# Regrouping the KV matmuls of a linear-attention kernel by array shape, and one identity made earlier

## The chip, the cores and the metric

The kernel runs on one core of one Trainium2 chip. The metric is the device time of one execution in microseconds (us), the median of several runs. Within a core five engines run side by side, each through its own instructions in order: TensorE (PE in the profile, its weight loads PEld), VectorE (DVE), ScalarE (ACT), GpSimd (POOL) and SyncE (SP). They wait for each other through semaphores.

## The reference, cut to what matters

Shapes: batch 8, heads 8, sequence 576, head dimension 64, features 128 (with both signs 256).

```python
def phi(x):
    proj = np.einsum('bhsd,df->bhsf', x, w_phi)
    proj = proj - np.max(np.abs(proj), axis=-1, keepdims=True)
    return np.concatenate([np.exp(proj), np.exp(-proj)], axis=-1)
q_p, k_p = (phi(q), phi(k))
kv = np.einsum('bhsf,bhsd->bhfd', k_p, v)
z = np.sum(k_p, axis=2)
num = np.einsum('bhsf,bhfd->bhsd', q_p, kv)
den = np.einsum('bhsf,bhf->bhs', q_p, z)[..., None] + 1e-06
x = num / den            # heads side by side: (8, 576, 512)
gate = 1 / (1 + exp(-causal_conv5(x, conv_w)))
out = (gate * (x @ w_val)) @ w_out
```

The KV sums are `kv` and `z`: for each batch, head and sign a product of 128 features by 65 columns (64 of v and a column that gives z), summed over 576 tokens.

## The kernel before, in words

A unit is two batches (b = 0, 1) and two heads (h = 0, 1); there are 16 units, four for each of the four pairs of batches. A unit's tokens lie in nine blocks of 128 partitions per head. The two batches have 576 tokens each, four blocks and a half, so blocks 0 to 3 belong to batch 0, blocks 5 to 8 to batch 1, and block 4 is shared: batch 0 in partitions 0 to 63, batch 1 in partitions 64 to 127.

The work is staged by hand. A step handles one of three groups (g = 0, 1, 2) of three blocks of a unit; each step issues its parts in the order `"KkTtNVxQLnaCvXqdc"`, in which capital letters stand for TensorE work and the others mostly for the engine that reads the result. In one step, for different units:

- K, k, x: `pe_K` (L260) projects keys into the PSUM tile PK; `max_K` (L268, VectorE) takes the row maxima MK; `exp_K` (L273, ScalarE) writes the key features KTIL with two exp activations, one for each sign.
- T, t: `pe_T` (L241, and L244 for the query maxima MQb) transposes the next group's KN and QN with the bf16 identity `ident_bf`; `copy_T` (L254, VectorE) copies to QKT.
- N, n: `pe_N` (L353) makes numerator and denominator NUM, `norm` (L361, L364, VectorE) divides, giving XN, seven steps behind K.
- V, v: `pe_KV` (L332, L335), once per unit, at the third group of the unit four steps back, makes the KV sums; `copy_KV` (L343, VectorE) copies them to KVSB in bf16.
- Q, q: `pe_Q` (L260, tile PA) and `max_Q` (L283, VectorE) make the query maxima MQb.
- L, a, d: the gated unit's work of a finished pair as a budget allows: GATE (L419), VAL (L440) and OP (L448) on TensorE, the tanh GS (L425) and the copy OS (L453) on ScalarE, the product GV (L429) on VectorE.
- C, c: `pe_C` (L306, L311, tile PQ) and `exp_C` (L318, ScalarE) make the query features QTIL, three steps behind K.
- X: once per pair, the transposes XP (L383) and their copies XT (L393, VectorE).

After the third group of a unit `emit_VT` lets GpSimd scale v by the keys' maxima: VT0 for the first sign, VT1 for the second (L294, L296).

PSUM is shared out in two pools: `ps2` has three buffers of two banks, which PK, PA, PQ, KV and GATE take in the order in which they are requested, and `ps1` two buffers of one bank, for T, NUM, XP, VAL and OP. A buffer can be written again once its last reader is done.

In `pe_KV` a two-bank tile holds batch 0 in one bank and batch 1 in the other, and in each bank four accumulators of 65 columns, n = 2h + sign. For each n the old order does four whole-array matmuls (128 partitions) for batch 0, four for batch 1, and then block 4: two matmuls on 64 partitions each, one for each batch, which take the upper and the lower half of the array. `start` clears the bank's flags, so that the first write to an accumulator overwrites.

At the start GpSimd issues the loads of unit 0 (`load_two(0)`, L123 and L129: four DMAs of KN, two of QN, four of VN), then makes the two identities `ident_bf` and `ident_f` (a memset and a select each, inside the helper masks.py), then issues unit 1's loads. VectorE makes EB (L166), ident_2 (L189) and DIAG (L195) from `ident_f`; TensorE transposes the convolution's weights with it (cwps, L192). This part stands ahead of the manual schedule, and the framework orders it by readiness.

Of the kernel before, what the change touches and what calls it, by code (L numbers as in the profile page):

```python
# [23 lines left out]
NC = NG * GC  # L24
# [32 lines left out]
def kernel(  # L57
# [24 lines left out]
    nc = tc.nc  # L82
# [14 lines left out]
    def half(h):  # L97
        return slice(h * D, h * D + D)

    def two_banks(name):  # L100
        return ps2.tile([P, 2, 512], FP32, name=name, tag="b2")
# [6 lines left out]
    for j, pr in enumerate(pairs):  # L108
        pr.j = j
        for hp in range(NHP):  # L110
            u = _Unit()
# [3 lines left out]
    def load_hps(j, tiles, hp0, nhp, dst0):  # L115
        QN, KN, VN = tiles
        h0, nh = 2 * hp0, 2 * nhp
        hs, ds = slice(h0, h0 + nh), slice(dst0, dst0 + nh)
        b0, b1 = 2 * j, 2 * j + 1
        lo, hi = slice(0, D), slice(D, P)  # L120
        def qload():
            for bb, ps in ((b0, lo), (b1, hi)):
                nc.gpsimd.dma_start(QN[ps, ds, :, :],  # L123
                                    q[bb, hs].rearrange("h (p c) d -> p h c d", c=NC))
        def kvload(T, x):
            for bb, ps, t0, nt, c0 in ((b0, lo, 0, 320, 0), (b0, hi, 320, 256, 0),
                                       (b1, lo, 0, 256, 5), (b1, hi, 256, 320, 4)):
                n = nt // D
                nc.gpsimd.dma_start(T[ps, ds, c0:c0 + n, :],  # L129
                                    x[bb, hs, t0:t0 + nt].rearrange("h (p c) d -> p h c d", c=n))  # L130
        kvload(KN, k)
        qload()
        kvload(VN, v)

    def load_two(i):

        u0, u1 = units[2 * i], units[2 * i + 1]
        tiles = [ldp.tile([P, 4, NC, D], BF16, name=n) for n in ("QN", "KN", "VN")]
        for w, u in enumerate((u0, u1)):
            u.QN, u.KN, u.VN = (t[:, 2 * w:2 * w + 2] for t in tiles)  # L140
        if i == 0:
            load_hps(u0.j, tiles, u0.hp, 1, 0)
            u1.load = lambda: load_hps(u1.j, tiles, u1.hp, 1, 2)
        else:
            load_hps(u0.j, tiles, u0.hp, 2, 0)


    load_two(0)
    ident_bf = const.tile([P, P], BF16, name="ident_bf")
    make_identity(nc, ident_bf[:])  # L150
    ident_f = const.tile([P, P], FP32, name="ident_f")
    make_identity(nc, ident_f[:])

# [169 lines left out]
    def pe_KV(u):  # L323
        KV = two_banks("KV")
        kvv = KV[:, :, 0:4 * (D + 1)].rearrange("p b (n e) -> p b n e", e=D + 1)
        for h in range(2):
            for sg in range(2):
                n = 2 * h + sg
                for b in range(2):
                    for c in range(4):  # L330
                        cc = c + 5 * b
                        nc.tensor.matmul(kvv[:, b, n, :], u.KTIL[:, sg, h * NC + cc, :], u.VT[sg][:, h * NC + cc, :],  # L332
                                         start=(c == 0), stop=False)
                for b in range(2):
                    nc.tensor.matmul(kvv[:, b, n, :], u.KTIL[half(b), sg, h * NC + 4, :],  # L335
                                     u.VT[sg][half(b), h * NC + 4, :],
                                     start=False, stop=True)
        u.KVps = kvv

    def copy_KV(u):  # L340
# [151 lines left out]
    def step(t):  # L492
# [18 lines left out]
        for o in ORDER:  # L511
            if o == "K" and u: pe_K(u, g)
            elif o == "k" and u: max_K(u, g)
            elif o == "x" and u: exp_K(u, g)
            elif o == "T" and (un or um): tt = pe_T(un, gn, um)
            elif o == "t" and (un or um): copy_T(un, um, *tt)
            elif o == "Q" and u: pe_Q(u, g)
            elif o == "q" and u: max_Q(u, g)
            elif o == "C" and uc: pe_C(uc, gc)
            elif o == "c" and uc: exp_C(uc, gc)  # L520
            elif o == "V" and uv and gv == 2: pe_KV(uv)
            elif o == "v" and uv and gv == 2: copy_KV(uv)
            elif o == "N" and ux: pe_N(ux, gx)
            elif o == "n" and ux:
                norm(ux, gx)
            elif o == "X" and uy and uy.hp == NHP - 1:
                for n in range(gy * GC, gy * GC + GC):
                    copy_X(uy.pair, n, pe_X(uy.pair, n))
                if gy == 1:
                    emit_virt(uy.pair, 0)  # L530
                if gy == 2:
                    emit_virt(uy.pair, 1)
                    ready[t + LAGM] = uy.pair
            elif o == "L":
                budget = min(budget + BUDGET[g], 45)
                while mlp and budget > 0:
                    cost, f = mlp.pop(0)
                    later.extend(f())
                    budget -= cost
            elif o == "a": run_later(ACT_)  # L540
            elif o == "d": run_later(DVE_)
# [46 lines left out]
```

## Time and profile before

| what | value |
|---|---|
| time, median of 3 runs | 280.35 us (279.16 to 280.41) |
| profiled execution | 279.15 us, of which 277.4 us are the span of the program's instructions |
| busy share of the span | TensorE 83%, VectorE 71%, ScalarE 66%, GpSimd 51% |
| TensorE instructions in all | 3488 matmuls, 3508 weight loads recorded |
| `pe_KV`, whole-array matmuls (L332) | 512, mean 198 ns each as drawn |
| `pe_KV`, half-row matmuls (L335) | 128, mean 203 ns each as drawn |
| VectorE's wait for the KV sums (L343) | 11.4 us in 16 waits |

The profile is that of one execution. A line of a timeline gives the start from the beginning of the span, the duration, the engine, the line of the kernel, the operation, the tile written and those read, the shape, and the number of instructions merged into it; a bracket at its end gives the idle time of the engine before it and what ended it. Matmuls are pipelined: each is drawn longer than the step from one start to the next, so TensorE's pace is read from starts. The chain of waits is followed back from the last instruction, at each step to what released it.

### The profile page before, as it was taken

To read this page: it belongs to the slowest core of one execution; us is meant where nothing else is said; L and a number is where in the kernel's file an instruction comes from. 1 tells how busy PE (TensorE), PEld (TensorE's weight loads), DVE (VectorE), ACT (ScalarE), POOL (GpSimd) and SP (SyncE) were. 2 spreads that over 40 slices of the span, in tenths; PEclk is the share of its full clock that TensorE was granted. 3 is DMA by queue.
4 is the path that set the end of the run, shared out by engine and by line. 5 is a ranking of instruction groups with operands and counts; after the bars stand their busy time and mean duration, and the time that the engine had idled before them with its cause. 6 is when DMAs were issued, how large, how long until landed. Compare 5 with 4: busy or idle time off the path is not lost.

```text
span 277.4 us, 8159 instructions
## 1 busy us (share of the span) xinstructions
PE 230.2 (83%) x3488; PEld 147.2 (53%) x3508; DVE 195.8 (71%) x346; ACT 182.7 (66%) x281; POOL 142.4 (51%) x195
## 2 busy tenths in 40 slices
PE   0478977777889989897899989998799989869992
PEld 0345755665655556575656464766546455533441
DVE  0798699999897667878897488778977554453211
ACT  1079798898666875979566786978648758202451
POOL 8999969969920946087714934143506051030000
PEclk9999999999999999999999999999999999988998
DMA  6999995934930497339900894411001503310445
GB/s 86 135 143 187 188 158 79 175 48 58 154 50 0 83 210 118 78 79 147 150 2 1 138 216 61 113 40 40 2 2 35 120 2 91 73 32 0 99 106 138
DMA packets 28990, 25.24 MB, mean 91 GB/s; under 512 B 2709, under 2 KB 24341, under 8 KB 28954
## 3 DMA queue, kind: packets, MB, share of 16 engines
q0 software_dynamic: 23024, 15.21, 39.9%
q1 hardware_dynamic: 5930, 9.52, 14.2%
q8 instruction: 27, 0.44, 0.7%
q14 instruction: 9, 0.07, 0.1%
HBM read 30.48 MB, written 9.44 MB: 144 GB/s over the span
## 4 chain that ended last, share of the span: by engine, by line
PE 55%; DVE 25%; ACT 12%; POOL 3%; issue 3%; POOLq 0%; ACTq 0%; DVEq 0%
PE OP L448 12%; PE GATE L419 8%; PE VAL L440 8%; PE KV L332 8%; DVE MK L268 8%; ACT KTIL L273 5%; DVE MQb L283 5%; PE NUM L353 4%; ACT QTIL L318 4%; DVE QKT L254 3%; PE KV L335 3%; PE XP L383 2%; PE PK L260 2%; PE T L241 2%; DVE GV L429 2%
## 5 line engine op out<-in xcount | busy, mean ns | idle before, releaser
L294 POOL TENSOR_TENSOR VT<-VN,E 128x1152 bf16<-128x1152 bf16 x32 | 68.7, 2149 | 78.5 <-issue 67.8
L273 ACT ACTIVATE KTIL<-PK 128x768 bf16<-128x768 f32 x96 | 73.1, 822 | 27.6 <-DVE MK L268 27.5
L318 ACT ACTIVATE QTIL<-PQ 128x768 bf16<-128x768 f32 x96 | 73.2, 826 | 18.9 <-PE PQ L311 18.9
L268 DVE TENSOR_REDUCE MK<-PK 128x6 f32<-128x768 f32 x48 | 45.9, 956 | 9.0 <-PE PK L260 8.9
L429 DVE SCALAR_TENSOR_TENSOR GV<-GS,VAL 128x512 bf16<-128x512 bf16 (+1 forms) x40 | 24.8, 633 | 37.8 <-ACT GS L425 32.8
L283 DVE TENSOR_REDUCE MQb<-PA 128x6 bf16<-128x768 f32 x48 | 45.6, 951 | 0.0
L448 PE MATMUL OP<-WOUT,GV 128*128 128x512 bf16 x124 | 33.9, 380 | 4.8 <-DVE QKT L254 3.3
L425 ACT ACTIVATE GS<-GATE 128x1024 bf16<-128x1024 f32 (+1 forms) x20 | 18.8, 939 | 26.0 <-PE GATE L419 25.6
L440 PE MATMUL VAL<-XT,WVAL 128*128 128x512 bf16 (+1 forms) x192 | 35.0, 329 | 0.0
L453 ACT ACTIVATE OS<-OP 128x512 f32<-128x512 f32 x36 | 21.8, 607 | 17.4 <-PE OP L448 13.3
L260 PEld LDWEIGHTS <-QKT 64*128 64x128 bf16 x576 | 20.1, 98 | 23.3 <-issue 13.5
L260 PE MATMUL PK<-W,QKT 64*128 64x128 bf16 x288 | 17.4, 229 | 16.5 <-ACT KTIL L273 10.3
L353 PE MATMUL NUM<-KVSB,QTIL 128*128 128x65 bf16 (+1 forms) x640 | 29.9, 196 | 0.5 <-DVE XT L393 0.3
L332 PE MATMUL KV<-VT,KTIL 128*128 128x65 bf16 x512 | 28.0, 198 | 0.0
L364 DVE TENSOR_TENSOR XN<-NUM,RCP 128x384 bf16<-128x384 f32 x48 | 26.8, 558 | 1.7
L254 DVE COPY QKT<-T 128x768 bf16<-128x768 bf16 (+2 forms) x49 | 27.5, 562 | 0.3 <-PE T L244 0.3
L353 PEld LDWEIGHTS <-QTIL 128*128 128x128 bf16 (+1 forms) x640 | 24.6, 100 | 3.2 <-issue 0.7
L419 PE MATMUL GATE<-XT,DIAG 64*64 64x512 bf16 (+1 forms) x480 | 24.6, 337 | 1.2 <-POOL XT L400 1.2
L440 PEld LDWEIGHTS <-WVAL 128*128 128x128 bf16 x192 | 14.9, 98 | 19.0 <-issue 7.5
L241 PE MATMUL T<-ident_bf,KN 128*128 128x128 bf16 x144 | 23.9, 236 | 0.0
L241 PE MATMUL T<-ident_bf,QN 128*128 128x128 bf16 x144 | 23.6, 235 | 0.0
L129 POOL DMA_DIRECT2D KN<-in_k_dram x36 | 22.7, 667 | 0.8 <-POOLq L572 0.8
(45 smaller groups left out, 298.2 us busy)
## 6 DMA issues: line engine op xcount, KB each, us to landing
out_dram<-OS SPq DMA_DIRECT2D x72, 128.0 KB, 2.4
QN<-in_q_dram POOLq DMA_DIRECT2D x14, 288.0 KB, 7.2
KN<-in_k_dram POOLq DMA_DIRECT2D x14, 160.0 KB, 4.5
VN<-in_v_dram POOLq DMA_DIRECT2D x14, 160.0 KB, 8.6
KN<-in_k_dram POOLq DMA_DIRECT2D x14, 128.0 KB, 4.4
VN<-in_v_dram POOLq DMA_DIRECT2D x14, 128.0 KB, 8.5
QN<-in_q_dram POOLq DMA_DIRECT2D x4, 144.0 KB, 3.7
WNAT<-in_moe_w_val_dram POOLq DMA_DIRECT2D x1, 512.0 KB, 6.2
```

The costliest lines, as they stand in the source:

```text
L241: nc.tensor.transpose(T[:, s * GC + i, :], src.rearrange("p h c d -> p (h c d)")[:, m * P:(m + 1) * P], ident_bf[:, :])
L260: nc.tensor.matmul(PA[:, r, i * P:(i + 1) * P], u.T[g][half(r), s, i, :], W2[half(r), :], start=True, stop=True)
L268: nc.vector.tensor_reduce(u.MK[:, :].rearrange("p (m r) -> p r m", r=2)[:, :, blocks(g)], u.PK, AX.X, ALU.max, apply_absolute_value=True)
L273: nc.scalar.activation(u.KTIL[:, sg].rearrange("p (m r) f -> p r m f", r=2)[:, :, blocks(g), :], u.PK, AF.Exp, scale=1.0 - 2.0 * sg)
L283: nc.vector.tensor_reduce(mq, u.PA, AX.X, ALU.max, apply_absolute_value=True, negate=True)
L294: nc.gpsimd.tensor_tensor(VT[:, :, 0:D], u.VN.rearrange("p h c d -> p (h c) d"), eb.to_broadcast([P, 2 * NC, D]), ALU.mult)
L318: nc.scalar.activation(u.QTIL[:, sg, :, :, g * GC * D:(g + 1) * GC * D], PQ[:, :, 0:GT].rearrange("p r (b x) -> p r b x", b=2), AF.Exp, sc ...
L332: nc.tensor.matmul(kvv[:, b, n, :], u.KTIL[:, sg, h * NC + cc, :], u.VT[sg][:, h * NC + cc, :], start=(c == 0), stop=False)
L353: nc.tensor.matmul(NUM[ps, i, h, :], u.QTIL[:, sg, r, b, m * D:m * D + ps.stop - ps.start], u.KVSB[:, b, 2 * h + sg, :], start=(sg == 0), ...
L419: nc.tensor.matmul(GATE[half(c), r, z * n:(z + 1) * n], DIAG[half(r), jt, tap, :], cols(jt, 4 - tap, half(r)), start=(tap == 0), stop=(tap ...
L440: nc.tensor.matmul(VL[:, z, :], WVAL[:, dt, v * P:(v + 1) * P], cols(dt, 0), start=(dt == 0), stop=(dt == 3))
L448: nc.tensor.matmul(OP[:, :], pr.GV[g][:, jt // 2, jt % 2, i * P:(i + 1) * P], WOUT[:, jt, :], start=(jt == 0), stop=(jt == 3))
```

## The change

In `pe_KV` all 32 whole-array matmuls of a unit come first, block by block (c), within a block over the four accumulators n, within these over the two batches b, so that successive matmuls write to alternating banks. The eight half-row matmuls come after them. `start` is set only for the first matmul into each bank. The numbers of matmuls and of weight loads are unchanged. Apart from this, `ident_bf` is made before `load_two(0)` in place of after it.

```diff
-    load_two(0)
     ident_bf = const.tile([P, P], BF16, name="ident_bf")
     make_identity(nc, ident_bf[:])
+    load_two(0)
     ident_f = const.tile([P, P], FP32, name="ident_f")
     make_identity(nc, ident_f[:])
...
     def pe_KV(u):
         KV = two_banks("KV")
         kvv = KV[:, :, 0:4 * (D + 1)].rearrange("p b (n e) -> p b n e", e=D + 1)
-        for h in range(2):
-            for sg in range(2):
-                n = 2 * h + sg
+
+        for c in range(4):
+            for n in range(4):
                 for b in range(2):
-                    for c in range(4):
-                        cc = c + 5 * b
-                        nc.tensor.matmul(kvv[:, b, n, :], u.KTIL[:, sg, h * NC + cc, :], u.VT[sg][:, h * NC + cc, :],
-                                         start=(c == 0), stop=False)
-                for b in range(2):
-                    nc.tensor.matmul(kvv[:, b, n, :], u.KTIL[half(b), sg, h * NC + 4, :],
-                                     u.VT[sg][half(b), h * NC + 4, :],
-                                     start=False, stop=True)
+                    cc = n // 2 * NC + c + 5 * b
+                    nc.tensor.matmul(kvv[:, b, n, :], u.KTIL[:, n % 2, cc, :], u.VT[n % 2][:, cc, :],
+                                     start=(c == 0 and n == 0), stop=False, skip_group_check=True)
+        for n in range(4):
+            for b in range(2):
+                cc = n // 2 * NC + 4
+                nc.tensor.matmul(kvv[:, b, n, :], u.KTIL[half(b), n % 2, cc, :], u.VT[n % 2][half(b), cc, :],
+                                 start=False, stop=True, skip_group_check=True)
         u.KVps = kvv
```

## The prediction

> **What bounds the kernel now.** I read the page's busy shares and chain first, then the list of waits, then the timeline of single engines around the KV sums, and the chain of waits at the start.
>
> ```profile
> PE 230.2 (83%) x3488; PEld 147.2 (53%) x3508; DVE 195.8 (71%) x346; ACT 182.7 (66%) x281; POOL 142.4 (51%) x195
> ...
> PE OP L448 12%; PE GATE L419 8%; PE VAL L440 8%; PE KV L332 8%; DVE MK L268 8%; ACT KTIL L273 5%; DVE MQb L283 5%; PE NUM L353 4%; ACT QTIL L318 4%; DVE QKT L254 3%; PE KV L335 3%; PE XP L383 2%; PE PK L260 2%; PE T L241 2%; DVE GV L429 2%
> ```
>
> TensorE is the fullest engine. L332 and L335 (8% and 3%) are 11% of the chain, 30 us, about all the time of the 16 KV sums: each lies on the chain. But the chain names only the last arrival; what comes second must be read too.
>
> TensorE in the KV sums of unit 6 (start, duration, instruction):
>
> ```profile
> 104.15 0.41 PE L332 MATMUL KV<-VT,KTIL 128*128 128x65 bf16 x8
> 104.50 0.20 PE L335 MATMUL KV<-VT,KTIL 64*128 64x65 bf16 x2
> 104.64 0.43 PE L332 MATMUL KV<-VT,KTIL 128*128 128x65 bf16 x8
> 104.99 0.21 PE L335 MATMUL KV<-VT,KTIL 64*128 64x65 bf16 x2
> ...
> 105.63 0.42 PE L332 MATMUL KV<-VT,KTIL 128*128 128x65 bf16 x8
> 105.98 0.20 PE L335 MATMUL KV<-VT,KTIL 64*128 64x65 bf16 x2
> 106.02 0.33 PE L260 MATMUL PA<-W,QKT 64*128 64x128 bf16 x6
> 106.29 0.63 PE L419 MATMUL GATE<-XT,DIAG 64*64 64x512 bf16 x8
> ```
>
> One matmul is drawn about 0.20 long, so the eighth of a group starts at 104.15 + 0.41 - 0.20 = 104.36: seven steps of 0.03 us. The two half-row matmuls start 0.14 later, not 0.03, and the next full one again 0.14 after them. A pair of half-row matmuls followed by others of half the rows (105.98 to 106.02) costs only 0.04. So the time sits in the changes between whole-array and half-row matmuls: seven per unit, 0.13 to 0.14 each.
>
> What else waits at that place, on ScalarE in unit 6 and unit 4, on TensorE in unit 4, and on VectorE in unit 1:
>
> ```profile
> 104.49 1.55 ACT L273 ACTIVATE KTIL<-PK 128x768 bf16<-128x768 f32 x2
> ```
> ```profile
> 72.06 1.51 ACT L273 ACTIVATE KTIL<-PK 128x768 bf16<-128x768 f32 x2 [1.01 <-DVE MK L268]
> ```
> ```profile
> 73.71 0.33 PE L306 MATMUL PQ<-QKT,W 64*128 64x384 bf16 x2
> ```
> ```profile
> 42.31 0.70 DVE L343 CAST KVSB<-KV 128x520 bf16<-128x520 f32 x1 [0.50 <-PE KV L335]
> 43.06 0.34 PE L260 MATMUL PK<-W,QKT 64*128 64x128 bf16 x6 [0.30 <-DVE KVSB L343]
> ```
>
> Two-bank PSUM tiles have three buffers. In a step with a KV sum they go to PK, KV, PA in turn, and the next (PQ or GATE) takes PK's, free when the second KTIL activation has read it: at 106.04 in unit 6, 0.25 before GATE starts, and at 73.57 in unit 4, 0.14 before PQ. TensorE starts some 0.05 after such a release (KVSB ends at 43.01, PK starts at 43.06). These are the second arrivals.
>
> **The change part by part: the KV matmuls.** The same 40 matmuls and 40 weight loads remain. Per unit three pairs of array changes go, 3 x (0.13 + 0.14) = 0.81; in their place stand three full steps, 3 x 0.03, and three half-row pairs, 3 x 0.04: 0.21. TensorE gains 0.60 of the 1.83 from the first to the last start. In unit 0 (29.18 to 31.93) TensorE steps at 0.054, changes cost 0.17 each, and a pair 0.05 to 0.10: 1.03 less 0.31 to 0.46, a gain of 0.57 to 0.72; I take 0.6. So 16 x 0.6 = 9.6 us of TensorE. The banks now alternate at each matmul; the old order changes bank between the fourth and fifth of each eight, inside the steps of 0.03, so I cost it at nothing. One clearing flag in place of four adds no instruction.
>
> [...]
>
> The third matmul now needs VT1; the old order had it wait until the eleventh. VT1 is ready at 24.8 for the sum at 29.18, and GpSimd's timeline shows 4.3 us or more for every unit: no wait.
>
> What of the 0.6 reaches the end, by unit (the second arrival in each):
> - Unit 0: VectorE waits 2.15 for KV, KTIL has ended at 31.19, PQ starts at 32.28: whole, 0.6.
> - Units 1 to 3: PQ can move only from 42.27 to 42.18 (KTIL ends at 42.13), but the query exp after it has 0.39 of room before the next key exp. The path goes on by KVSB, MQb, MK to ScalarE. VectorE's wait is 0.50, and its starts overlap by 0.08: 0.55 each, 1.65.
> - Units 4, 8, 12: PQ moves to 73.57 + 0.05 = 73.62, and XP behind it on TensorE, for which VectorE waits: 0.09 each, 0.27.
> - Units 5, 9, 13: PA, then two output matmul groups that use one-bank tiles; PQ at 92.53 is far behind KTIL's end at 90.83; ScalarE waits 0.94 for OP. Whole, 1.8.
> - Units 6, 10: GATE moves to 106.04 + 0.05 = 106.09 and no further: 0.2 each, 0.4.
> - Units 7, 11: KTIL ends at 120.39, GATE starts at 121.11: whole, 1.2.
> - Units 14, 15: no keys are left, VectorE waits 1.09 for KV: whole, 1.2.
>
> Sum 7.1. The other 2.5 us become a TensorE wait for KTIL (units 4, 6, 8, 10, 12) and a full VectorE (1 to 3).
>
> **The change part by part: the identity.** The start of the chain of waits:
>
> ```profile
> 0.63 0.61 issue
> 1.24 2.56 POOL KN L129 x4
> ...
> 7.65 0.39 POOL ident_bf masks.py:199
> 8.04 0.25 POOL ident_f masks.py:199
> 8.29 0.02 issue
> 8.31 1.34 DVE EB L166
> ```
>
> Two memsets and two selects take GpSimd's queue from 7.25 to 8.17, when the next load is issued. One identity alone: 0.40 from memset to select (it waits for the memset), 0.28 to the next instruction, 0.68. Ahead of the loads some of it fits into the 0.61 of issue, so ten load issues come 0.07 to 0.68 late, I take 0.35. ident_f then ends at 7.25 + 0.35 + 0.40 + 0.39 = 8.39 in place of 8.28: 0.1 late (bounds -0.2 and +0.45), and the EB copies, with a VectorE that has no gap until 20.7, carry that to the end. The first transposes (8.85 to 9.67) come 0.35 later at most 0.7; their copy starts at 11.26 behind EB, so 1.5 us cover it. Without that cover it would cost the whole delay. The later loads shift by the same 0.1.
>
> Forecast: 7.1 - 0.1 = 7.0 us. The profiled execution took 279.15 (span 277.4 and 1.75 around it), so it would be 272.1. It is the low one of the three runs; from the median of 280.35 the forecast is 273.3, rounded to 273.2.
>
> **The rivals.**
> - *All of it passes* (0.15). If the two-bank buffers fall differently, so that GATE and PQ take one that is free sooner, the full 9.6 comes through: 280.35 - 9.6 = 270.7. For it: the buffers are given at build time. Against it: PQ and GATE wait for ScalarE's semaphore, and the order of requests is unchanged.
> - *The start is reordered* (0.12). Work ahead of the manual schedule is ordered by readiness (the memsets of MQb run before the copy of W though written after it). If the copy of T then stands before EB on VectorE, it waits for the transposes to about 9.85 in place of 8.31: 1.5 us lost, 274.8. Against it: TensorE already put the four cwps transposes ahead of T, as if T were bound by its loads, which come no sooner.
> - *The slow pace lasts* (slower; 0.05). TensorE's six T transposes take 0.82 until 28.5 and 0.51 from 33.2 on, with a granted clock of 1.00 in both. The pace rises inside a stretch without a gap, from 28.02 to 34.4, which the change shortens by 0.6. If it then stayed slow through units 1 to 3, TensorE's 7.5 busy us of a 10.1 us period would become 7.5 x 0.82/0.51 = 12: 1.9 us lost in each unit on top of the gain. From about four such units (7.0/1.9) the kernel is slower, up to 282. Against it: the rise came 4 to 5 us into the stretch, of which 5.8 are left.
> - *Nothing happens* (0.03): the change cost is not between array shapes but, say, a semaphore update on the half-row matmuls, and stays; 280.3. Against it: half-row pair to PA shows no such step.
>
> [...]
>
> **How the numbers follow.** Forecast 0.65, the rivals 0.15, 0.12, 0.05, 0.03. Range: low end is the whole gain with the start's best bound (9.8) and half the runs' spread of 1.2: 270.0; high end takes the start's loss of 1.5, its upper bound of 0.45 and a third of a us less in each of units 5, 7, 9, 11, 13: 276.8. About 0.5% (1.4 us) is what a measurement of this kernel can tell from no change. Faster by more: all of the first three, some of the mixed cases lost: 0.91; within it 0.05; slower 0.04.
>
> **What the new profile would show.** Right: a KV sum of 1.23 us in place of 1.83, one jump of 0.13 in it; VectorE's wait for KV down from 0.50 to about zero in units 1 to 3; a new TensorE wait for ACT KTIL of 0.4 to 0.5 ahead of PQ in units 4, 8, 12 and GATE in 6 and 10; EB at 8.4. Wrong: full steps above 0.03, no wait for KTIL there, EB behind the first QKT copy, or T at 0.82 after 33.

## The result, and the profile after

| | before | changed |
|---|---|---|
| median | 280.38 us (279.16 to 282.16, 4 runs) | 270.41 us (270.11 to 272.90, 4 runs) |
| profiled execution | 279.15 us, span 277.4 | 272.90 us, span 271.1 |
| ratio | | 0.9695, 95% interval 0.9648 to 0.9742 |

The changed kernel is faster by 3%; the forecast was 273.2 us, with a range of 270.0 to 276.8. To read the difference of the two medians, 10.0 us, one has to know that in some executions of either kernel TensorE's granted clock is halved for one or more stretches of 3.4 us (0.50 from 247.96 to 251.37 in the profile before, from 46.95 to 50.36, 57.19 to 60.60 and 67.43 to 70.84 in the changed one), so that executions are best compared at equal clock. Over all runs of the two kernels, the executions with a mean clock of 0.995 or more took 277.65 to 278.35 us before (22 of 45 beside the experiments, middle 277.9) and 270.07 to 270.53 changed (7 of 16, middle 270.3): 7.6 us.

The page of the changed kernel, its busy shares and its chain:

```profile
PE 222.6 (82%) x3488; PEld 144.3 (53%) x3508; DVE 195.0 (72%) x346; ACT 182.9 (67%) x281; POOL 142.7 (53%) x195
...
PE OP L448 12%; ACT KTIL L273 9%; PE GATE L419 8%; PE VAL L440 8%; DVE MK L268 8%; ACT QTIL L318 6%; DVE MQb L283 4%; PE KV L331 4%; PE NUM L353 4%; DVE QKT L254 3%; PE XP L383 3%; PE PQ L306 3%; DVE GV L429 2%; ACT GS L425 2%; PE T L241 2%
```

The KV sums (now L331 and L336) have fallen from 11% of the chain to 5% (L331 4%, L336, which the page no longer lists, 0.9%), and the key exp KTIL has risen from 5% to 9%: in many units the chain no longer passes through the KV sum but through what was second. Which arrival takes its place differs between executions: in a later profile of the same kernel KTIL has 5% and the key maxima MK 11%. TensorE's timeline in units 6 and 4, and ScalarE's in unit 6:

```profile
103.69 1.14 PE L331 MATMUL KV<-VT,KTIL 128*128 128x65 bf16 x32
104.76 0.29 PE L336 MATMUL KV<-VT,KTIL 64*128 64x65 bf16 x8
104.89 0.33 PE L260 MATMUL PA<-W,QKT 64*128 64x128 bf16 x6
105.64 0.63 PE L419 MATMUL GATE<-XT,DIAG 64*64 64x512 bf16 x8 [0.41 <-ACT KTIL L273]
```
```profile
73.92 0.34 PE L306 MATMUL PQ<-QKT,W 64*128 64x384 bf16 x2 [0.42 <-ACT KTIL L273]
```
```profile
104.03 1.55 ACT L273 ACTIVATE KTIL<-PK 128x768 bf16<-128x768 f32 x2
```

From the first full matmul to PA are 1.20 us in place of 1.87. There is one jump, from the last full start (103.69 + 1.14 - 0.20 = 104.63) to 104.76. And GATE, which used to follow PA at once, now starts 0.06 after KTIL has ended at 105.58; PQ in unit 4 waits in the same way. VectorE's waits for KV show the same from the other side; here the line's own view in that later profile (e8_after_third):

```profile
L343 DVE CAST KVSB<-KV x16: 689/692/700, 32.0 to 229.2; 128x520 bf16<-128x520 f32 x16
...
  PE KV L336: 2.3, 3
```

Before it was 11.4 us in 16 waits; the three that are left are those of units 0, 14 and 15. The start, in the chain of waits:

```profile
0.73 0.21 POOL ident_bf masks.py:197
0.94 0.31 issue
1.25 0.04 POOLq masks.py:199
1.29 0.77 POOL KN L129
...
2.15 0.31 POOL ident_bf masks.py:199
2.46 1.73 POOL KN L129 x3
...
7.75 0.21 POOL ident_f masks.py:197
7.96 0.52 POOL KN L129
8.48 0.32 POOL ident_f masks.py:199
8.80 0.02 issue
8.83 1.34 DVE EB L166
```

The early identity is split by a load's issue, and so is ident_f: a load of unit 1 now stands between its memset and its select. EB starts at 8.83 in place of 8.31.

### The profile page after: what moved, and what is told of

Same layout as the page of the kernel before. It is cut to its first block, busy times and chain, and to the rows that moved or that the text cites. A ratio compares the mean times of both kernels' runs of the same rounds, so it can differ in the third digit from the quotient of the medians.

```text
span 271.1 us, 8159 instructions
## 1 busy us (share of the span) xinstructions
PE 222.6 (82%) x3488; PEld 144.3 (53%) x3508; DVE 195.0 (72%) x346; ACT 182.9 (67%) x281; POOL 142.7 (53%) x195
## 4 chain that ended last, share of the span: by engine, by line
PE 49%; DVE 24%; ACT 19%; POOL 3%; issue 3%; POOLq 0%; ACTq 0%; DVEq 0%
PE OP L448 12%; ACT KTIL L273 9%; PE GATE L419 8%; PE VAL L440 8%; DVE MK L268 8%; ACT QTIL L318 6%; DVE MQb L283 4%; PE KV L331 4%; PE NUM L353 4%; DVE QKT L254 3%; PE XP L383 3%; PE PQ L306 3%; DVE GV L429 2%; ACT GS L425 2%; PE T L241 2%
## 5 line engine op out<-in xcount | busy, mean ns | idle before, releaser
L260 PEld LDWEIGHTS <-QKT 64*128 64x128 bf16 x576 | 20.5, 100 | 21.8 <-issue 12.6
L260 PE MATMUL PK<-W,QKT 64*128 64x128 bf16 x288 | 18.0, 236 | 14.8 <-ACT KTIL L273 8.9
L353 PEld LDWEIGHTS <-QTIL 128*128 128x128 bf16 (+1 forms) x640 | 25.3, 102 | 3.2 <-issue 0.7
L419 PE MATMUL GATE<-XT,DIAG 64*64 64x512 bf16 (+1 forms) x480 | 23.6, 327 | 2.2 <-POOL XT L400 1.2
L241 PE MATMUL T<-ident_bf,KN 128*128 128x128 bf16 x144 | 24.5, 241 | 0.0
L241 PE MATMUL T<-ident_bf,QN 128*128 128x128 bf16 x144 | 24.3, 239 | 0.0
L400 POOL COPY XT<-XT 128x504 bf16<-128x504 bf16 x16 | 9.3, 618 | 26.1 <-DVE XT L393 26.1
```

The lines of the kernel that those rows point to most:

```text
L241: nc.tensor.transpose(T[:, s * GC + i, :], src.rearrange("p h c d -> p (h c d)")[:, m * P:(m + 1) * P], ident_bf[:, :])
L260: nc.tensor.matmul(PA[:, r, i * P:(i + 1) * P], u.T[g][half(r), s, i, :], W2[half(r), :], start=True, stop=True)
L353: nc.tensor.matmul(NUM[ps, i, h, :], u.QTIL[:, sg, r, b, m * D:m * D + ps.stop - ps.start], u.KVSB[:, b, 2 * h + sg, :], start=(sg == 0), ...
L419: nc.tensor.matmul(GATE[half(c), r, z * n:(z + 1) * n], DIAG[half(r), jt, tap, :], cols(jt, 4 - tap, half(r)), start=(tap == 0), stop=(tap ...
```

## The experiments

**The changed kernel twice more.** No edit; in the first profile of the changed kernel units 1 to 3 lay at half clock in places.

> The changed kernel as it is, for a second profile and more times beside the kernel before. The profile of its first look had a mean granted clock of 0.977 with dips to 0.7 between 47 and 75 us, and its times without a profile were 270.1 to 270.5. Theory A (second arrivals as predicted, the surplus over the forecast of 7.0 is granted clock): with a clock of 0.99 or more in both profiles units 1 to 3 have periods of 9.5 to 9.6 us in place of 10.1, units 4, 8, 12 still 16.8, units 6, 10 still 13.7, the part up to the end of the KV sums shrinks by 7 us, and what remains of the 10 us lies where the kernel before had a lower clock, in its tail after 234 us. Theory B (more passes than predicted): the units 1 to 3 gain over 0.6 each, or the tail after the last KV sum is shorter at an equal clock.

> The changed kernel a third time, as the base for the two beside it: 270.2 us in executions with a granted clock of 0.995 or more, 1.2 to 1.4 us more for each stretch of 3.4 us at half clock.

Measured: 271.40 us median (270.20 to 273.06) and 271.91 (270.07 to 273.17), before beside them 279.07 and 277.97; ratios 0.9742 (0.9692 to 0.9793) and 0.9747 (0.9698 to 0.9797). The time from one unit's first KV matmul to the next one's, from TensorE's timelines, before and in the last of these profiles (e8_after_third):

| units | before | changed | gain of one | forecast |
|---|---|---|---|---|
| 0 | 11.05 | 10.37 | 0.68 | 0.6 |
| 1, 2, 3 | 10.11, 10.10, 11.23 | 9.53, 9.53, 10.64 | 0.58 | 0.55 |
| 4, 8, 12 | 16.88 | 16.80 | 0.08 | 0.09 |
| 5, 9, 13 | 15.60, 15.59, 14.76 | 14.92, 14.92, 14.09 | 0.67 | 0.6 |
| 6, 10 | 13.86 | 13.67 | 0.19 | 0.2 |
| 7, 11 | 13.84 | 13.17 | 0.67 | 0.6 |
| 14 | 10.70 | 10.03 | 0.67 | 0.6 |

These add up to 7.1. What comes after the last KV sum's start depends on the clock. With two stretches of half clock that begin 10.0 to 10.5 us after it, it took 43.4 or 43.5 in the old order (in the kernels with the identity alone and with the flags and banks alone, below) and 42.8 with the regrouped sums, 0.6 less, as forecast; where the two begin 12.3 or 12.6 after it, two kernels with regrouped sums (in the second profiles below) took 43.7 and 43.8. Without half clock it took 41.1 changed and 42.7 in the kernel with twice as many array changes (below): 1.61 more, which is what that kernel's KV sum is longer. Theory A holds in the main: of the 3.0 us by which the medians' difference exceeds the forecast, 2.4 are clock, since 7.6 remain at equal clock. Theory B falls: units 1 to 3 gain under 0.6 each, and the end gains no more than the last KV sum.

**The regrouped KV sums alone, and the early identity alone.** The first is the changed kernel with

```diff
-    ident_bf = const.tile([P, P], BF16, name="ident_bf")
-    make_identity(nc, ident_bf[:])
     load_two(0)
+    ident_bf = const.tile([P, P], BF16, name="ident_bf")
+    make_identity(nc, ident_bf[:])
```

and the second the kernel before with the opposite edit.

> The regrouped KV sums alone; the identity is made after the first loads, as before. Theory A: in the changed kernel a load issue came between the memset and the select of ident_f, which ended at 8.80 in place of 8.28, and the EB copies and all of VectorE's start with it; undone, the kernel is 0.5 us faster than the changed one, about 269.9 us where that one is 270.4. Rival: the start is covered by later waits, and the time is the same within 0.2 us.

> The regrouped KV sums alone again; in its first turn all six executions had a clock of 0.983 to 0.990. Theory A (those were chance, the identity costs 0.5 us): executions at 0.995 or more take 269.7 us. Rival (this kernel's start lets a half-clock stretch fall into the tail every time): again no execution above 0.99, and a median of 271.7, no better than the changed kernel.

> The early bf16 identity alone, with the KV sums in the old order. Theory A: 0.5 us slower than the kernel before (EB starts at 8.83 in place of 8.31), about 280.9 us where before is 280.4. Rival (the early identity brings part of the surplus, by earlier transposes or another start): 1 to 2 us faster than before.

Measured: the identity alone 279.63 us (278.28 to 281.05, 12 runs), before beside it 279.07, ratio 1.0021 (0.9990 to 1.0052). The executions at 0.995 or more took 278.28 to 278.40 (4) and 279.16 (1), before 277.9: 0.5 us slower in the middle one. In its profile the first KV matmul starts at 29.68 in place of 29.18, and the periods after it are those of before except where half clock falls into them. That is what theory A says, though the ratio alone would not show it. The KV sums alone: 271.81 us (271.63 to 272.64), ratio 0.9756 (0.9719 to 0.9792), and the second time 271.66 (269.92 to 274.36), with a ratio of 0.9729 (0.9682 to 0.9777) for the four executions at a clock of 0.989 or more. Medians do not separate them from the changed kernel, since 11 of 12 executions had a clock under 0.995; the one at 0.996 took 269.92, against 270.3. In both profiles the start reads as before:

```profile
8.04 0.25 POOL ident_f masks.py:199
8.29 0.02 issue
8.31 1.34 DVE EB L166
```

The first KV matmul starts at 29.18 and 29.19 in place of 29.70, and the periods after it are the same, but for those with half clock in them. So the whole gain is the KV sums', and the early identity takes back 0.4 to 0.5 us. Whether the clock was low in 11 of 12 by chance stays open.

**New flags and banks, old array changes.** For each accumulator the eight full matmuls go through the banks in turn, with the half-row pair after them; the identity is made after the loads, as before, here and in the next two kernels:

```diff
-        for c in range(4):
-            for n in range(4):
+        for n in range(4):
+            for c in range(4):
                 for b in range(2):
...
-        for n in range(4):
             for b in range(2):   # the half-row pair, inside the loop over n
```

> The new flags and the new alternation of banks at each matmul, but with the half-row matmuls after each eight full ones, as before, so that all seven array changes remain; the identity is made after the loads. Theory A (the array changes are the cost): a KV sum takes 1.83 us from the first to the last start, as before, and the time is that of the kernel before within 0.3%. Rival (the four clearing flags, or four matmuls in a row into one accumulator, are the cost): the KV sum shrinks to near 1.2 us and the time falls by most of the 10 us.

```profile
103.96 0.41 PE L331 MATMUL KV<-VT,KTIL 128*128 128x65 bf16 x8
104.30 0.20 PE L335 MATMUL KV<-VT,KTIL 64*128 64x65 bf16 x2
104.44 0.42 PE L331 MATMUL KV<-VT,KTIL 128*128 128x65 bf16 x8
104.79 0.20 PE L335 MATMUL KV<-VT,KTIL 64*128 64x65 bf16 x2
```

Measured: 278.03 us (277.38 to 280.23), ratio 0.9991 (0.9955 to 1.0026). All seven jumps are there, and a KV sum takes 1.80 us. Clearing flags and banks are not the cost. At equal clock it is 0.5 us faster than before (277.4 against 277.9): 15 sums after the first are each shorter by 0.03, and each period after the first is shorter by 0.03 to 0.04. Which of the two, flags or banks, gives the 0.03 was not separated.

**Twice as many array changes.** Each half-row matmul follows its own batch's four full ones:

```diff
+        for n in range(4):
+            for b in range(2):
+                for c in range(4):
...
+                nc.tensor.matmul(kvv[:, b, n, :], u.KTIL[half(b), n % 2, cc, :], ...)
```

> Each half-row matmul follows the four full ones of its own batch, so that a KV sum has eight short half-row stretches in place of four; flags as in the changed kernel, identity after the loads. Theory A (a change into half-row matmuls and back costs 0.26 to 0.27 us whatever else is there): four more changes each way, one pair turned into two single ones, so a KV sum of about 1.83 + 4 x 0.24 = 2.8 us from first to last start; nothing covers a longer sum, so nearly all of 16 x 0.96 = 15 us arrives: about 293 us beside 278 clean before. Rival (the cost is per pair or per accumulator, not per change): the sum stays at 1.83 and the time at 278.

```profile
110.11 0.29 PE L331 MATMUL KV<-VT,KTIL 128*128 128x65 bf16 x4
110.33 0.20 PE L334 MATMUL KV<-VT,KTIL 64*128 64x65 bf16 x1
110.46 0.30 PE L331 MATMUL KV<-VT,KTIL 128*128 128x65 bf16 x4
110.69 0.20 PE L334 MATMUL KV<-VT,KTIL 64*128 64x65 bf16 x1
```

Measured: 297.38 us (294.81 to 299.62), with a ratio of 1.0572 (1.0495 to 1.0649) for the two executions at a clock of 0.984 or more (294.81 and 295.37). No execution reached 0.995, where about 293 was expected. A KV sum takes 2.78 us, 0.13 or 0.14 at each change as before, and each period between units 1 and 13 is longer by 0.93 to 0.95, the whole of it. A single half-row matmul pays what a pair pays: the price is that of the change, not of the pair or the accumulator. Why a change costs this, no run shows.

**PK's buffer free earlier.** In each unit's first group, which falls into the steps with a KV sum, the second key exp reads the first one's result, so that the second sign's features of that group are wrong; it handles as many elements.

```diff
-                u.PK, AF.Exp, scale=1.0 - 2.0 * sg)
+            src = part[0] if sg == 1 and g == 0 else u.PK
+            nc.scalar.activation(part[sg], src, AF.Exp, scale=1.0 - 2.0 * sg)
```

> Regrouped KV sums, identity after the loads, and in the steps with a KV sum the second key exp reads the first one's result in SBUF in place of PK, so that PK's buffer is free 0.7 us earlier (this changes what is computed: the second sign's key features of one group in three are wrong). Theory A (PK's buffer, held until the second key exp, is the second arrival that stops 0.41 us of the gain in units 4, 6, 8, 10, 12): the waits of TensorE for KTIL ahead of PQ and GATE are gone there, and the periods of units 4, 8, 12 fall from 16.8 to about 16.4 and of 6, 10 from 13.67 to about 13.3: 2 us less than the same kernel without it. Rival (something else would hold it at the same point, VectorE or the transposes): periods unchanged within 0.1.

```profile
70.31 0.29 PE L336 MATMUL KV<-VT,KTIL 64*128 64x65 bf16 x8
70.44 0.33 PE L260 MATMUL PA<-W,QKT 64*128 64x128 bf16 x6
70.61 0.33 PE L306 MATMUL PQ<-QKT,W 64*128 64x384 bf16 x2
```

Measured: 266.56 us (265.88 to 268.04), ratio 0.9557 (0.9503 to 0.9610). In unit 4 PQ follows PA at once, with no wait. The periods of units 4, 8, 12 fall from 16.80 to 16.20 or 16.21, those of 6, 10 from 13.67 to 13.13, the rest stays within 0.1 (unit 3 apart, with a stretch of half clock). The two exps take no less time than before (69.63 to 71.31, 1.68 us, against 1.51 to 1.55), so it is the buffer and not a shorter exp. The first KV matmul also starts 0.59 earlier than with the KV sums alone (28.59 against 29.18), since a wait of PK for KTIL at the start is gone too; the expectation left that out. The mechanism is shown; its size was set too small, since the wait of 0.41 begins in the trace only where PA is drawn to end: PQ's start moved from 0.75 to 0.17 after PA's, 0.58.

**An earlier start.** Both identities ahead of the loads, and, in a further kernel, also the values of units 1 to 3 after the keys and queries of units 2 and 3:

```diff
     make_identity(nc, ident_bf[:])
-    load_two(0)
     ident_f = const.tile([P, P], FP32, name="ident_f")
     make_identity(nc, ident_f[:])
+    load_two(0)
... from here on the further kernel alone
-    units[1].load()
+    units[1].load("kq")
...
     load_two(1)                 # now its keys and queries alone
+    units[1].load("v")
+    units[2].load()             # the values of units 2 and 3
```

> The changed kernel with both identities ahead of the first loads. ident_f is then ready at about 1.6 us in place of 8.8, and EB, ident_2 and DIAG fill VectorE's idle time before 8 us. Theory A (VectorE bounds the first 20 us, so its 4.4 us of work at the start are saved): 2 us faster than the changed kernel, clean 268.1. Rival (the next bound is the loads: in the kernel before TensorE already waited 0.2 us at 25.6 for queries that landed at 25.7, and these loads come no sooner): 0.2 to 0.6 us faster, clean 269.6 to 270.

> Both identities first, and the values of unit 1 and of units 2 and 3 loaded after the keys and queries of units 2 and 3, whose queries are then issued about 2.5 us sooner. Theory A (after the identities the loads of those queries bound the start): 1 to 2 us faster than with both identities first alone, clean about 268. Rival (GpSimd's value scaling of unit 0 or 1 then waits for its values, and the KV sums with it): no gain, or a loss up to 2 us, with a new TensorE wait for VT in unit 0 or 1.

> Regrouped KV sums, both identities first, and the values of units 1 to 3 after the keys and queries of units 2 and 3, again, beside the changed kernel on the same chip. Theory A: executions at a clock of 0.995 or more take 268.2 us, 2.0 less than the changed kernel, and the median is lower by 1 to 2. Rival: the gain of the first turn was a matter of clock, and the difference is under 0.5.

TensorE with both identities first:

```profile
23.64 0.29 PE L241 MATMUL T<-ident_bf,KN 128*128 128x128 bf16 x1
25.95 0.26 PE L241 MATMUL T<-ident_bf,QN 128*128 128x128 bf16 x1 [2.02 <-DMA QN<-in_q_dram]
```

Measured: 270.43 us (268.40 to 271.68), ratio 0.9678 (0.9627 to 0.9730). In the profile the rival is right: TensorE comes to these transposes 2.4 us earlier and then waits 2.0 for the queries; the first KV matmul starts at 29.31, 0.39 earlier than in the changed kernel. But the only execution at 0.995 took 268.40, near theory A's 268.1 and below the rival's 269.6. No run shows whether the queries landed sooner there, so the two stay undecided. With the values later: 270.20 (268.18 to 271.15), ratio 0.9672 (0.9626 to 0.9717), and the second time 269.65 (268.31 to 271.12), ratio 0.9678 (0.9634 to 0.9721), against 0.9747 for the changed kernel beside it. The first KV matmul starts at 27.2 to 27.4, and the three executions at 0.995 or more took 268.18 to 268.50 against 270.3: 2.0 us, theory A of the second time. That the later values gain 1 to 2 us over both identities first, as theory A of the first time has it, is not shown: the medians are 270.20 and 270.43 on one chip, and the single executions at 0.995 or more 268.18 and 268.40. The rival's wait appears too, small: in unit 1 of the second profile VT1 is ready at 37.9 for a KV sum that starts at 37.74, which takes 1.35 us. This kernel has the lowest medians of those with the whole computation.

## Why the prediction was right, and where it was off

- *The cost of an array change* was right: 0.13 and 0.14 us in every profile with changes, and doubled with their number.
- *The KV sum's gain* was set at 0.60 and measured 0.66 to 0.67 (1.83 or 1.84 to 1.17 or 1.18, first start to last). The term that was off is the half-row pair: three pairs in 0.09 us (104.76 + 0.29 - 0.20 = 104.85), 0.03 and not 0.04 each; and the alternating banks and fewer clearing flags, costed at nothing, together gained 0.03 a sum in the experiment on them.
- *What passes* was right unit by unit, within 0.08 in every row of the table. The second arrival, PK's buffer, gives units 4, 6, 8, 10, 12 their small gains, and taking it away gave 0.54 to 0.60 more in each. The step that decided the forecast was reading, for each unit, not the chain but which event would come next.
- *The identity* was set at a cost of 0.1 with bounds of -0.2 and 0.45, and costs 0.5, at or just beyond the upper bound. The delay of the loads was about right (the first values' issue at 5.32 in place of 4.92, 0.40). What failed is "ident_f then ends at 8.39": the prediction kept the memset and the select together, and a load's issue came between them, so that the select started 0.74 after the memset (7.66 to 8.40), not 0.40.
- *Unit 0's KV sum and VT1*: no TensorE wait for VT in the changed kernel, as said.
- *From profile to median*: the forecast carried the 7.0 us to the median of three runs, all of which, at 279.16 and more, lie above every execution at 0.995 or more (278.35 at most), so probably with halved stretches (the profiled one has one, and a mean clock of 0.990). Three of the four executions of the changed kernel had none. By the counts above, where about half of either kernel's executions have none, that is luck: 2.4 of the 10.0 us come from it, and it is why the median of 270.41 lies nearer to the 270.7 of the rival than to the forecast. (280.35 - 7.0 is 273.35; the prediction wrote 273.2.) Sum of the rows: 7.1 + 0.6 - 0.5 = 7.2; executions at equal clock give 7.6. The last 0.4 is not located.
- *The rivals*: "all of it passes" would have been 9.6 and fell with the waits for KTIL; the reordered start did not occur (QKT still stands behind EB); the slow pace ended at 33.3, 31.9 and 33.0 in the three profiles, before at 32.9, so it did not last.

The KV sum's gain rests on the step within the run of 32 full matmuls, each with a weight load of its own (512 loads for 512 matmuls on L331). In unit 6 it is 0.03 us ((104.63 - 103.69) / 31), as within the eights of the order before ((104.36 - 104.15) / 7).

## What to carry to other kernels

Look at start times around each change of a matmul's array shape: here a change cost as much as four full matmuls of 65 columns (0.13 us against 0.03 each), and sorting the KV sum by shape, with one clearing flag for a bank, took six of its seven changes out and 0.66 of its 1.83 us, with the same 40 matmuls. Before counting the gain, look for the next arrival at each place: the buffer that rotates, and who reads it last. And do not split a short pair of dependent instructions from the work that waits for it when something is moved within a queue: here one load's issue slipped in between, EB started 0.52 later (8.83 against 8.31) and the kernel took 0.4 to 0.5 longer.

## What the runs showed of the hardware that was not expected

In these profiles the granted clock fell to half (0.50) for whole stretches of 3.41 us, on a grid of that length counted from the first rise (33.3 in the changed kernel's first profile; 46.95 is four steps later), in 16 of 17 cases after a stretch in which TensorE was busy for little more than half (1.80 to 2.12 us as drawn). In all 13 profiles every change of the clock lies a whole number of steps after the first rise. Stretches from the windows of the changed kernel, for TensorE alone (length, busy time, granted clock, DMA), and of the kernel before, for all engines (length, busy TensorE, weight loads, VectorE, ScalarE, GpSimd, granted clock, DMA):

```profile
43.54:46.95 3.41, 2.11 (x44) 1.00 0.21 22
46.95:50.36 3.41, 2.94 (x41) 0.50 1.15 151
50.36:53.77 3.41, 3.10 (x88) 1.00 1.18 183
53.77:57.19 3.42, 2.01 (x44) 1.00 1.26 176
57.19:60.60 3.41, 2.93 (x41) 0.50 0.10 16
...
241.51:244.92 3.41, 1.97 (x25) 1.00 0.00 0
244.92:248.34 3.42, 3.42 (x31) 1.00 0.00 0
```
```profile
244.55:247.96 3.41, 1.81 (x20) 1.34 (x21) 2.50 (x8) 0.00 (x0) 1.54 (x3) 1.00 0.00 0
247.96:251.37 3.41, 3.14 (x22) 1.06 (x22) 0.00 (x0) 0.62 (x1) 0.77 (x2) 0.50 0.00 0
```

Of the 17 falls from full to half clock in the 13 profiles, ahead of the last matmul, 16 followed a stretch with 1.80 to 2.12 us of TensorE time, as drawn, and one a stretch with 3.00 (236.29 in the kernel with twice as many changes). But no threshold of the drawn busy time comes out: 34 stretches with 1.89 to 2.12 were followed by full clock, as that with 1.97 above. What else decides stays open. Where the grid lies against the kernel differs between executions (in the three profiles of the changed kernel the rise comes at 33.3, 31.9 and 33.0 and the first KV matmul at 29.7), which would explain why either kernel falls into it in about half of them; no experiment set the grid. The longest single TensorE wait inside the first of these stretches is 0.90 us, so the fall after it followed no longer idle. The columns for the time before the first rise read 1.00, though the T transposes run at half pace there (0.11 us from start to start before it, 0.055 after); the starts of matmuls are the safer reading.

The price of a change is not one of the KV sums alone. In the kernel before, at full clock, PA starts 0.125 to 0.127 us after the last whole-array matmul of NUM (0.03 from step to step within NUM; 28 places), T starts 0.147 to 0.149 after the last half-row matmul of PK (0.05 from pair to pair within PK; 40 places), and PQ 0.310 to 0.312 after the last 512-column matmul of OP (0.216 within OP; 11 places). In each of them, as in the KV sums, the change adds 0.09 to 0.10 us to the step.
